# The first chunk's early hidden columns kept in DRAM and multiplied by w_out at the end of layer 1

## The chip, the cores and the metric

The kernel runs on one core of a Trainium2 chip. Its time is the time on the device of one execution, in microseconds (us). A core has five engines that work side by side, each through its own queue in order: TensorE (PE) multiplies matrices, VectorE (DVE) and ScalarE (ACT) work element by element, GpSimd (POOL) does so too, and SyncE (SP) issues the transfers between DRAM and the core's memory (SBUF). PE writes to eight accumulator banks (PSUM). An instruction waits until what it reads is written and what it overwrites is no longer needed; what stands behind it on its queue waits with it.

## The reference

```python
scores = scale * np.matmul(q, k.transpose(0, 1, 3, 2))    # batch 4, heads 8, 576 x 64
Dmat = np.where(rel >= 0, gamma[:, None, None] ** rel[None, :, :], 0.0)
attn = np.matmul(scores * Dmat, v)
x = np.ascontiguousarray(attn.transpose(0, 2, 1, 3)).reshape(B * S, H * D)   # 2304 x 512
g = x @ w_gate                                            # 512 x 1536
x = (g * (1.0 / (1.0 + np.exp(-g))) * (x @ w_val)) @ w_out     # 1536 x 512
h = np.maximum(x @ w_in, 0.0)                             # 512 x 2048
return (h * h) @ w_out2                                   # 2048 x 512
```

A retention without softmax gives 2,304 tokens of 512 channels; two layers follow, a gated one (1,536 hidden columns) and one with a squared ReLU (2,048). The weights arrive as 64-bit floats.

## The kernel before

All tokens stand in SBUF as `xy` (128 partitions, 4 blocks of channels, 2,304 tokens). A matrix product in full precision is made of three fast ones: each operand is split into a rounded part and a rest (`split`: ACT casts the first, DVE subtracts for the second), and `three` multiplies high by high, high by low and low by high.

**Weights.** A 64-bit weight tile of 128 x 512 is a *unit*. `conversion` turns the 68 units into 32 bits, in the order of the list `order`: a load (`raw`), two steps on ACT, four or five on DVE, a store to DRAM (`wst`). `pump` advances it step by step; `ensure` runs it until a wanted unit is there. While the attention runs, `UNITS_EARLY` units are done; behind it `PACE` steps go with each product.

**The attention** takes 16 pairs (batch, two heads) one after the other. A pair n has scores, states, and the outputs of pair n - 2, copied to `xy` by ACT out of one bank `o`; its last 64 tokens go through a piece of a bank `s`. The flag `chain` fixes the order of each engine's instructions there to that of the program, for what is written inside. From pair 6 on each pair also takes one projection (`hidden0`) of the *first chunk*, the first 448 tokens: 12 matmuls for gate or value of one of the first six of twelve column blocks f. The split hidden tiles stay in SBUF (`hs`).

**Layer 1** behind it. `out0` multiplies the six stored hidden tiles by w_out: 72 matmuls into four banks, saved to DRAM as `part`. The other work is done in *passes*. A pass (1, 0), (1, 1), (2, 0), ... takes two blocks of tokens (464 each in layer 1, 384 in layer 2) and multiplies 2 x 2 blocks of weights by 2 x 2 blocks of tokens with seven products in place of eight (`slot` i = 1 to 7, six matmuls each). One such product over two column blocks is a *system* n. The token operands `xo_h`, `xo_l` of product i come from `renew` (sums of blocks of `xy` on DVE, then a split), the weight operands `wi` from `build`: GpSimd makes the sums (`stationary`: s1 and three in place), ACT and DVE split them, and the first pass of a layer stores them as `win` for the later ones. The pass (1, "rest") takes the first chunk with the other six column blocks, by plain products (`plain_slot`, 24 matmuls of 448 columns a system). `out1` and `out2` multiply hidden tiles `ho_hi`, `ho_lo` by w_out tiles `wo` (a pool of four, two to a pair of column blocks; `load_out` loads one and splits it) and add into `xy`.

Outside `chain` a scheduler sets the order on each engine, by its own estimate of times; each engine then runs that order. Before, the passes of layer 1 run (1, 0), "rest", (1, 1); `part` is loaded into `xy` in "rest".

Of the kernel before, what the change touches and what calls it, by code (L numbers as in the profile page):

```python
# [61 lines left out]
def retention_moe_kernel(  # L62
# [64 lines left out]
    order = [(1, what, f) for f in range(HALF) for what in "gv"] + [(1, "o", f) for f in range(HALF)]  # L127
# [164 lines left out]
    hs, gates = {}, {}  # L292

    def hidden0(k):
# [13 lines left out]
        hs[f] = (hi, lo)  # L308

    acc = []  # L310
    part = part_p.tile([P, CC, M0], F32, tag="part", name="part")

    def out0(f):

        if f == 0:
            acc.extend(ps_a.tile([P, 512], F32, tag=f"a{i}", name=f"a{i}")[:, :M0] for i in range(CC))
        ensure((1, "o", f), units)
        w, h = units.pop((1, "o", f)), hs.pop(f)
        for cc in range(CC):
            three(acc[cc], cut(w, cc * P, P), h, f == 0, f == HALF - 1)  # L320
        if f < HALF - 1:
            return
        for cc, a in enumerate(acc):
# [4 lines left out]
            sp.dma_start(out=part[:, cc, :], in_=dst)

    with ExitStack() as st:  # L330
# [11 lines left out]
        pairs = [(b, hp) for b in range(B) for hp in range(NP)]  # L342
# [181 lines left out]
    tt = dve.tensor_tensor  # L524


    passes = list(TOKENS)
    systems = [
        (ph, p, k, what)
        for ph, p in passes  # L530
        for k in range(HALF // 2 if p == "rest" else 0, (F1, F2)[ph - 1] // 2)
        for what in ("gv", "i")[ph - 1]
    ]
    win = {
        (ph, k, what, x): part_p.tile([P, 2, 256 * len(r)], F32, tag=f"win{ph}{what}{k}{x}", name="win")
        for ph, p, k, what in systems if p == 0 for x, r in enumerate(ROWS)
    }
    xo = {}

    def renew(at, i):  # L540


        m = M[at[0]]
        if at[1] == "rest":
            m, src = M0, xy[:, 2 * i - 2:2 * i, :M0]
        else:
            b11, b12, b21, b22 = (xy[:, c:c + 2, t:t + m] for c in (0, 2) for t in TOKENS[at])
            b31, b41 = b11, b21
            if at == (1, 1) and i in (7, 4):
                b31 = b41 = temp("bv", 2)  # L550
            if i == 5:
                tt(out=b12, in0=b12, in1=b11, op=ALU.subtract)
            elif i == 6:
                tt(out=b12, in0=b22, in1=b12, op=ALU.subtract)
            elif i == 7:
                tt(out=b31, in0=b12, in1=b11, op=ALU.subtract)
            elif i == 4:
                tt(out=b41, in0=b21, in1=b12, op=ALU.subtract)
            src = {1: b11, 2: b21, 3: b22, 4: b41, 5: b12, 6: b12, 7: b31}[i]
        hi, lo = (xo_p.tile([P, 2, M[1]], F32R, tag=f"x{x}{i}", name=f"xo_{x}") for x in "hl")  # L560
        xo[i] = hi[:, :, :m], lo[:, :, :m]
        split(*xo[i], src)

    def temp(tag, rows):
        return c4_p.tile([P, rows, M[1]], F32, tag=tag, name=f"c{tag}")

    sys_, built = {}, {}

    inputs = {}

    def load_in(n):
        ph, p, k, what = systems[n]
        inputs[n] = [in_p.tile([P, 512], F32, tag=f"in{x}", name="w_in") for x in range(2)]
        for x, w in enumerate(inputs[n]):
            ensure((ph, what, 2 * k + x), stored)
            sp.dma_start(out=w, in_=wst[ph, what, 2 * k + x])

    def operand_tile(n, x):
        w = wi_p.tile([P, 2, 256 * len(ROWS[x])], F32R, tag=f"wi{x}", name="wi")
        for at, i in enumerate(ROWS[x]):  # L580
            built[n, i] = w[:, :, 256 * at:256 * at + 256]
        return w

    def build(n):

        ph, p, k, what = systems[n]
        if p not in (0, "rest"):
            for x in (0, 3, 2, 1):
                w = operand_tile(n, x)
                sp.dma_start(out=w.bitcast(F32), in_=win[ph, k, what, x])  # L590
                yield
                if x != 2:
                    yield
            return
# [327 lines left out]
```

## Time and profile before

| | us |
|---|---|
| median of 3 runs | 918.2 (915.24 to 922.93) |
| the profiled execution | 920.45 |
| its span, first to last instruction | 918.7 |
| PE busy | 884.8 (96%) |
| DVE busy | 679.3 (74%) |
| ACT busy | 438.6 (48%) |
| POOL busy | 103.3 (11%) |
| transfers, mean rate over the span | 221 GB/s |
| mean granted clock of PE, of 1 | 0.985 |

The busy time of PE is the time in which any matmul was under way. A matmul takes as long again at the lower of PE's two clock levels (1.2 and 2.4 GHz), and counts as busy all the same; the granted clock of a stretch is the mean of the two in parts of the higher. Times below are from the start of the span.

### The profile page before, as it was taken

The page shows a single profiled execution, that of the slowest core. Times are in us where ns is not written, and L with a number is a line of the kernel's source. Part 1 is how long each engine was busy: PE and PEld are TensorE (multiplying, and loading weights), DVE is VectorE, ACT ScalarE, POOL GpSimd, SP SyncE. Part 2 cuts the span into 40 slices and gives each one's busy share as a digit, 9 for nine tenths or more (in the row PEclk, how much of TensorE's full clock was granted, in tenths as well). Part 3 has the DMA queues.
Part 4 walks back from the last instruction along what each step waited for, and adds up shares of the span by engine and source line. Part 5 has one row for each costly group of instructions (what it writes and reads, how often), then busy time and mean ns, then how long its engine had stood idle before and what let it go on. Part 6 is the DMA issues. An engine that isn't in the chain of part 4 may idle for free.

```text
span 918.7 us, 13809 instructions
## 1 busy us (share of the span) xinstructions
PE 884.8 (96%) x5050; PEld 782.0 (85%) x5050; DVE 679.3 (74%) x1098; ACT 438.6 (48%) x781; POOL 103.3 (11%) x119
## 2 busy tenths in 40 slices
PE   7899959899999999899999999999999999999998
PEld 6688848788888899788888999989999999998986
DVE  3777887879989998877877899668754568554553
ACT  3555555675656655455543547534433334243220
POOL 2121160323303000000000223200000000000000
PEclk9999989899999999999999999999999999999999
DMA  8888557998879757889985457534664454554402
GB/s 327 280 277 292 160 196 234 358 318 283 296 258 305 277 190 252 261 302 330 317 289 194 152 200 253 199 140 148 204 197 127 160 171 161 171 184 155 141 3 69
DMA packets 83076, 202.85 MB, mean 221 GB/s; under 512 B 8512, under 2 KB 20288, under 8 KB 83008
## 3 DMA queue, kind: packets, MB, share of 16 engines
q1 hardware_dynamic: 83008, 201.97, 65.3%
q8 instruction: 40, 0.66, 0.3%
q14 instruction: 28, 0.23, 0.1%
HBM read 141.77 MB, written 60.16 MB: 220 GB/s over the span
## 4 chain that ended last, share of the span: by engine, by line
PE 71%; DMA 11%; DVE 10%; issue 3%; ACT 3%; POOL 1%; SPq 1%; ACTq 0%; DVEq 0%; POOLq 0%
PE oacc L116 29%; PE g L116 20%; PE v L116 11%; DMA raw<-in_w 6%; PE z L116 4%; DVE w L116 3%; PE o L116 3%; PE s L116 3%; DVE wi L116 2%; DMA w_in<-wst 1%; DVE xy L116 1%; DMA wst<-w 1%; DMA win<-wi 1%; DVE xo_l L116 1%; DMA kv_sb<-in_kv 1%
## 5 line engine op out<-in xcount | busy, mean ns | idle before, releaser
L116 PE MATMUL g<-xo_h,wi 128*128 128x464 f32 (+2 forms) x816 | 251.1, 359 | 9.4 <-ACT wi L116 3.3
L116 PE MATMUL oacc<-wo,ho_hi 128*128 128x512 f32 x576 | 181.0, 392 | 0.0
L116 PEld LDWEIGHTS g<-xo_h,wi 128*128 128x128 f32 x816 | 153.6, 190 | 23.9 <-ACT cbg L116 4.0
L116 PE MATMUL g<-xo_l,wi 128*128 128x464 f32 (+2 forms) x408 | 146.1, 358 | 0.0
L116 PE MATMUL v<-xo_h,wi 128*128 128x464 f32 (+2 forms) x432 | 136.8, 359 | 7.9 <-ACT wi L116 5.3
L116 PE MATMUL oacc<-ho_hi,wo 128*128 128x464 f32 (+1 forms) x432 | 138.5, 372 | 0.5 <-DVE xy L116 0.5
L116 PEld LDWEIGHTS oacc<-wo,ho_hi 128*128 128x128 f32 x576 | 107.3, 188 | 17.6
L116 DVE TENSOR_TENSOR xy<-oacc,xy 128x464 f32<-128x464 f32 (+2 forms) x146 | 94.3, 650 | 33.8 <-PE oacc L116 33.6
L116 PE MATMUL oacc<-wo,ho_lo 128*128 128x512 f32 x288 | 112.6, 392 | 0.0
L116 PEld LDWEIGHTS v<-xo_h,wi 128*128 128x128 f32 x432 | 80.8, 189 | 15.5 <-ACT wi L116 5.7
L116 PEld LDWEIGHTS oacc<-ho_hi,wo 128*128 128x128 f32 x432 | 81.0, 188 | 10.1 <-DVE xy L116 0.9
L116 DVE TENSOR_SCALAR w<-w 128x512 f32<-128x512 f32 (+1 forms) x136 | 58.6, 431 | 37.2 <-ACT w L116 36.4
L116 PEld LDWEIGHTS g<-xo_l,wi 128*128 128x128 f32 x408 | 77.7, 191 | 6.4
L116 PE MATMUL oacc<-ho_lo,wo 128*128 128x464 f32 (+1 forms) x216 | 80.1, 371 | 0.0
L116 ACT ACTIVATE raw<-raw 128x512 uint32<-128x512 uint16 x68 | 45.9, 675 | 68.6 <-DMA raw<-in_w 62.8
L116 PE MATMUL v<-xo_l,wi 128*128 128x464 f32 (+2 forms) x216 | 77.2, 357 | 0.0
L116 DVE TENSOR_TENSOR wo<-wo 128x512 fp32r<-128x512 f32 x78 | 54.2, 708 | 16.5 <-ACT wo L116 16.3
L116 DVE TENSOR_TENSOR cbg<-v,cbg 128x384 f32<-128x384 f32 (+1 forms) x72 | 41.7, 579 | 30.1 <-ACT cbg L116 19.4
L116 PEld LDWEIGHTS oacc<-wo,ho_lo 128*128 128x128 f32 x288 | 54.1, 188 | 11.5
L116 ACT CAST wo<-wo 128x512 fp32r<-128x512 f32 x78 | 47.4, 622 | 32.5 <-DMA wo<-wst 31.7
L116 ACT CAST wi<-w_in 128x512 fp32r<-128x512 f32 x72 | 44.1, 618 | 38.2 <-POOL w_in L116 9.2
L116 PE MATMUL z<-xo_h,wi 128*128 128x464 f32 (+1 forms) x192 | 61.8, 360 | 0.2 <-DVE cag L116 0.2
(100 smaller groups left out, 1366.6 us busy)
## 6 DMA issues: line engine op xcount, KB each, us to landing
wi<-win SPq DMA_DIRECT2D x84, 512.0 KB, 4.2
raw<-in_w SPq DMA_DIRECT2D x68, 512.0 KB, 5.0
win<-wi SPq DMA_DIRECT2D x60, 512.0 KB, 4.3
wo<-wst SPq DMA_DIRECT2D x78, 256.0 KB, 4.2
wst<-w SPq DMA_DIRECT2D x68, 256.0 KB, 5.2
w_in<-wst SPq DMA_DIRECT2D x52, 256.0 KB, 4.1
qk_sb<-in_qk SPq DMA_DIRECT2D x15, 576.0 KB, 5.8
kv_sb<-in_kv SPq DMA_DIRECT2D x15, 576.0 KB, 4.4
```

The lines of the kernel that those rows point to most:

```text
L116: i = op(*args, **kw)
```

## The change

- `out0`, its banks and `part` go. `hidden0` stores its split tiles to DRAM (`h_st`, two stores of 224 KB for each of the six). In the "rest" pass `early_hidden` loads them back, and `out1` multiplies them there, with 12 more additions or copies into `xy`; their w_out units become ordinary `wo` tiles.
- The passes of layer 1 run (1, 0), (1, 1), "rest". The token blocks change: (1, 0) takes the tokens from 448 and 1,840, (1, 1) those from 912 and 1,376, (2, 0) those from 768 and 1,920, which the "rest" pass does not write.
- The attention takes the batches in the order 0, 3, 1, 2, so that the tokens of (1, 0) are there by pair 13. In pairs 14 and 15 the operands 1 and 5 of the first system are made, in pairs 14 to 17 its weight operands, inside `chain`.
- `WA` 14 to 8, `UNITS_EARLY` 14 to 13, and the 24 steps of conversion between the `out0` go.

```diff
-    (1, 0): (M0 + M[1], M0 + 2 * M[1]),
+    (1, 0): (M0, M0 + 3 * M[1]),
+    (1, 1): (M0 + M[1], M0 + 2 * M[1]),
     (1, "rest"): (0,),
-    (1, 1): (M0, M0 + 3 * M[1]),
-    **{(2, p): (M[2] * p, NT // 2 + M[2] * p) for p in range(NT // (2 * M[2]))},
+    (2, 0): (2 * M[2], 5 * M[2]),
...
+SOON = (1, 5)
+BATCHES = (0, 3, 1, 2)
...
-WA = 14
+WA = 8
...
-UNITS_EARLY = 14
-
-PUMPS = {0: 1, "out": 4}
+UNITS_EARLY = 13
+
+PUMPS = {0: 1}
...
         split(hi, lo, t)
-        hs[f] = (hi, lo)
+        for x, part in enumerate((hi, lo)):
+            sp.dma_start(out=h_st[f // 2, x][:, f % 2], in_=f32(part))
...
-        pairs = [(b, hp) for b in range(B) for hp in range(NP)]
+        pairs = [(b, hp) for b in BATCHES for hp in range(NP)]
...
             if nxt:
                 prep_state(n + 1)
+            if n == 13:
+                load_in(0)
+            if n == 14:
+                make = build(0)
+                renew((1, 0), 1)
+            if n == 15:
+                renew((1, 0), 5)
+            if n >= 14:
+                next(make, None)
+                next(make, None)
+        for _ in make:
+            pass
...
+    def early_hidden(k):
+        parts = [ho_p.tile([P, 2, M0], F32R, tag=f"{x}b", name="ho_e") for x in "hl"]
+        for x, t in enumerate(parts):
+            sp.dma_start(out=t.bitcast(F32), in_=h_st[k, x])
+        hid[rest + 2 * k, "b"] = parts
...
+    for k in range(HALF // 2):
+        plan(rest + 1 + k, rest + 2 * k, "b", k)
+        fetch.setdefault(rest + k, []).append((1, range(2 * k, 2 * k + 2)))
+    for x, (at, n) in enumerate(((4, 1), (5, 3), (6, 5))):
+        plan(rest + at, rest + n, "a")
+        fetch.setdefault(rest + at - 1, []).append((1, range(HALF + 2 * x, HALF + 2 * x + 2)))
...
         if n == 0:
-            load_in(0)
             load_in(1)
-            for _ in build(0):
-                pass
-            seq = [("out", 0), ("out", 1), (1, n), ("out", 2), (5, n), ("out", 3), (6, n), ("out", 4), ("out", 5), (2, n)]
-            for i in (1, 5, 6, 2):
+            for i in (6, 2, 7, 4, 3):
                 renew(passes[0], i)
+            seq = [(1, n), (5, n), (2, n), (6, n)]
...
-        if (n, p) == (systems.index((1, "rest", HALF // 2, "g")) + 1, "rest"):
-            sp.dma_start(out=xy[:, :, :M0], in_=part)
+        if rest <= n < rest + HALF // 2:
+            early_hidden(n - rest)
+        for j in {rest + 3: (5, 6, 3), rest + 4: (7,), rest + 5: (4,)}.get(n, ()):
+            renew((2, 0), j)
```

**The order, first excerpt: ACT ahead of the attention's last banks.** Numbers tell buffers apart; `xy<-o` is the copy of the bank `o`, `raw` and `w<-raw` are the first steps of a unit's conversion, `w_hi` the high part of a weight or hidden tile. Before, from the copy of pair 13's bank to that of pair 14's:

```order
L116 COPY xy_78<-o_1385 128x512
L116 CAST w_hi_1406<-w_1298 128x512
L116 COPY sb_1421<-kvs_1412 128x64
L116 CAST w_hi_1441<-t_1356 128x448
L116 COPY xy_78<-s_1402 128x64
L116 ACTIVATE raw_1296<-raw_1296 128x512
L116 ACTIVATE w_1452<-raw_1296 128x512
L116 COPY xy_78<-o_1455 128x512
```

In the changed kernel, up to the copy of pair 14's bank (`o_1583`):

```order
L120 CAST wi_1749<-w_in_1706 128x512
L120 COPY xy_78<-o_1499 128x512
L120 CAST w_hi_1520<-w_1404 128x512
L120 COPY sb_1535<-kvs_1526 128x64
L120 ACTIVATE raw_1752<-raw_1752 128x512
L120 CAST w_hi_1555<-t_1462 128x448
L120 COPY xy_78<-s_1516 128x64
L120 CAST xo_h_1567<-xy_78 128x928
L120 CAST wi_1573<-s1_1478 128x256
L120 ACTIVATE raw_1402<-raw_1402 128x512
L120 ACTIVATE w_1580<-raw_1402 128x512
L120 COPY xy_78<-o_1583 128x512
```

Between the two copies there now stand, besides what was there, a cast of system 1's weights before them, the first step of the next unit (`raw_1752`), and the casts of operand 5 (`xo_h_1567`) and of a weight sum (`wi_1573`).

**Second excerpt: PE behind the last projection** (`v<-xh, w_hi`; `a0` to `a3` are the banks of `out0`; `g`, `v` and `z` those of the products). Before:

```order
L116 MATMUL v_1532<-xl_601,w_hi_1472 128x448
L116 MATMUL v_1532<-xh_600,w_lo_1473 128x448
L116 MATMUL a0_1710<-w_hi_731,w_hi_1520 128x448
L116 MATMUL a0_1710<-w_lo_732,w_hi_1520 128x448
L116 MATMUL a1_1711<-w_hi_731,w_hi_1520 128x448
L116 MATMUL a1_1711<-w_lo_732,w_hi_1520 128x448
L116 MATMUL a2_1712<-w_hi_731,w_hi_1520 128x448
L116 MATMUL a2_1712<-w_lo_732,w_hi_1520 128x448
L116 MATMUL a3_1713<-w_hi_731,w_hi_1520 128x448
L116 MATMUL a3_1713<-w_lo_732,w_hi_1520 128x448
L116 MATMUL g_1766<-xo_h_1688,wi_1669 128x464
L116 MATMUL g_1766<-xo_l_1689,wi_1669 128x464
```

In the changed kernel, where six matmuls of system 1 (`g_1806` with `wi_1749`) also stand ahead of the attention's last `s` bank, and five of `g_1737` ahead of these rows:

```order
L120 MATMUL g_1737<-xo_h_1474,wi_1480 128x464
L120 MATMUL v_1759<-xo_h_1567,wi_1573 128x464
L120 MATMUL v_1759<-xo_l_1568,wi_1573 128x464
L120 MATMUL v_1759<-xo_h_1567,wi_1573 128x464 x2
L120 MATMUL v_1759<-xo_l_1568,wi_1573 128x464
L120 MATMUL v_1759<-xo_h_1567,wi_1573 128x464
L120 MATMUL z_1768<-xo_h_1715,wi_1480 128x464
L120 MATMUL g_1806<-xo_h_1711,wi_1798 128x464
L120 MATMUL g_1737<-xo_h_1711,wi_1631 128x464
L120 MATMUL g_1737<-xo_l_1712,wi_1631 128x464
L120 MATMUL g_1737<-xo_h_1711,wi_1631 128x464 x2
L120 MATMUL g_1737<-xo_l_1712,wi_1631 128x464
```

The matmuls of `out0` are gone; products 1 and 5 of system 0 follow the projection, and then products 2 and 6 begin, whose operands are `xo_h_1715` and `xo_h_1711`, `xo_l_1712`.

**Third excerpt: PE in the "rest" pass,** `oacc` being the banks of `out1`. Before, from the last matmul of `wo_3418`, whose place `wo_3794` takes; that one is first used 47 rows later:

```order
L116 MATMUL oacc_3703<-ho_hi_3522,wo_3418 128x464
L116 MATMUL oacc_3703<-ho_hi_3522,wo_3422 128x464
L116 MATMUL oacc_3703<-ho_lo_3523,wo_3422 128x464
L116 MATMUL oacc_3703<-ho_hi_3522,wo_3422 128x464
L116 MATMUL oacc_3736<-ho_hi_3595,wo_3635 128x448
L116 MATMUL oacc_3736<-ho_lo_3596,wo_3635 128x448
L116 MATMUL oacc_3736<-ho_hi_3595,wo_3635 128x448
L116 MATMUL oacc_3736<-ho_hi_3595,wo_3639 128x448
L116 MATMUL oacc_3736<-ho_lo_3596,wo_3639 128x448
L116 MATMUL oacc_3736<-ho_hi_3595,wo_3639 128x448
L116 MATMUL g_3848<-xo_h_3334,wi_3817 128x448 x2
L116 MATMUL g_3848<-xo_l_3335,wi_3817 128x448
```

In the changed kernel, right behind the last matmul of `wo_4784`, whose place `wo_4917` takes:

```order
L120 MATMUL oacc_5112<-ho_hi_4884,wo_4788 128x464
L120 MATMUL oacc_5112<-ho_lo_4885,wo_4788 128x464
L120 MATMUL oacc_5112<-ho_hi_4884,wo_4788 128x464
L120 MATMUL g_5272<-xo_l_4676,wi_5195 128x448
L120 MATMUL g_5272<-xo_h_4675,wi_5195 128x448 x2
L120 MATMUL g_5272<-xo_l_4676,wi_5195 128x448
L120 MATMUL g_5272<-xo_h_4675,wi_5195 128x448
L120 MATMUL g_5272<-xo_h_4711,wi_5195 128x448
L120 MATMUL g_5272<-xo_l_4712,wi_5195 128x448
L120 MATMUL g_5272<-xo_h_4711,wi_5195 128x448 x2
L120 MATMUL g_5272<-xo_l_4712,wi_5195 128x448
L120 MATMUL oacc_5120<-ho_e_4925,wo_4917 128x448
```

The tile that takes a freed place is now wanted 12 rows later.

## Rows read from the trace of the kernel before

**Rows 1.** Stretches behind the attention: PE, PEld, DVE, ACT, POOL busy (count), PEclk, DMA, GB/s.

```profile
118.55:164.46 45.91, 34.93 (x151) 28.82 (x151) 37.24 (x56) 24.27 (x45) 15.54 (x10) 0.89 0.69 227
164.46:189.56 25.10, 21.77 (x92) 18.97 (x92) 22.84 (x34) 16.99 (x33) 10.18 (x11) 0.86 1.01 351
189.56:288.55 98.99, 98.48 (x470) 87.62 (x468) 88.98 (x148) 59.94 (x106) 25.70 (x27) 1.00 0.84 288
288.55:364.90 76.35, 74.40 (x358) 66.72 (x357) 72.93 (x117) 43.43 (x69) 2.62 (x3) 1.00 0.77 255
364.90:402.39 37.49, 34.88 (x160) 31.01 (x159) 29.95 (x52) 19.29 (x33) 0.00 (x0) 0.95 0.83 285
402.39:523.79 121.40, 120.76 (x578) 107.92 (x576) 95.20 (x161) 63.45 (x109) 5.89 (x7) 1.00 0.76 261
523.79:918.70 394.91, 390.29 (x1945) 351.69 (x1943) 250.82 (x366) 149.06 (x255) 21.38 (x24) 1.00 0.47 157
```

**Rows 2.** Chain that ended last: start, duration, what, matmuls.

```profile
338.92 2.44 PE v L116 x12
...
486.00 2.51 PE g L116 x12
```

**Rows 3.** PE in order of time: start, duration, instruction, idle before and its releaser.

```profile
113.50 0.87 PE L116 MATMUL o<-qs,sb 64*64 64x128 f32 x12
...
118.19 0.36 PE L116 MATMUL v<-xh,w_lo 128*128 128x448 f32 x1
...
134.25 0.76 PE L116 MATMUL v<-xo_h,wi 128*128 128x464 f32 x1 [5.27 <-ACT wi L116]
...
169.31 0.75 PE L116 MATMUL g<-xo_h,wi 128*128 128x464 f32 x1 [3.33 <-ACT wi L116]
...
383.21 0.76 PE L116 MATMUL g<-xo_h,wi 128*128 128x464 f32 x1 [2.61 <-ACT cbg L116]
```

**Rows 4.** ACT in order of time, at the end of the attention.

```profile
101.76 0.91 ACT L116 ACTIVATE kv_sb<-kv_sb,ks_sb 128x256 f32<-128x256 f32 x2
...
109.24 0.56 ACT L116 CAST w_hi<-t 128x448 fp32r<-128x448 f32 x1 [3.45 <-DVE t L116]
...
110.97 0.57 ACT L116 COPY xy<-o 128x512 f32<-128x512 f32 x1
...
115.92 3.57 ACT L116 CAST xo_h<-xy 128x928 fp32r<-128x928 f32 x4
```

**Rows 5.** DVE in order of time, same stretch.

```profile
102.74 1.22 DVE L116 TENSOR_TENSOR p_sb<-s,mask_sb 128x1024 f32<-128x1024 f32 x1 [1.57 <-PE s L116]
...
108.59 0.61 DVE L116 TENSOR_TENSOR t<-v,t 128x448 f32<-128x448 f32 x1
...
111.05 1.12 DVE L116 TENSOR_TENSOR xy<-xy 128x928 f32<-128x928 f32 x1
...
116.93 3.73 DVE L116 TENSOR_TENSOR xo_l<-xy,xo_h 128x928 fp32r<-128x928 f32 x3 [1.49 <-ACT xo_h L116]
```

**Rows 6.** Groups by shape: count, busy us, mean ns, idle before.

```profile
L116 DVE TENSOR_TENSOR wi<-w_in,wi 128x512 fp32r<-128x512 f32 x72 | 52.8, 738 | 3.1 <-ACT wi L116 2.8
...
L116 ACT ACTIVATE raw<-raw 128x512 uint32<-128x512 uint16 x68 | 45.9, 675 | 68.6 <-DMA raw<-in_w 62.8 <-DVE cag L116 2.2 <-DVE xy L116 1.6
...
L116 POOL TENSOR_TENSOR w_in<-w_in 128x256 f32<-128x256 f32 x40 | 38.9, 973 | 11.7 <-DMA w_in<-wst 9.1
```

**Rows 7.** SP issuing transfers, in order of time.

```profile
94.65 0.33 SPq L116 DMA_DIRECT2D kv_sb<-in_kv  x1
...
104.63 0.33 SPq L116 DMA_DIRECT2D raw<-in_w  x1
```

**Rows 8.** Transfers on the page: count, size, median us from issue to landing.

```profile
raw<-in_w SPq DMA_DIRECT2D x68, 512.0 KB, 5.0
...
wo<-wst SPq DMA_DIRECT2D x78, 256.0 KB, 4.2
```

**Rows 9.** POOL in order of time, behind the attention.

```profile
125.29 5.36 POOL L116 TENSOR_TENSOR w_in<-s,w_in 128x256 f32<-128x256 f32 x1 [4.03 <-DVE wi L116]
```

More of the change, by code (lines that the diff above doesn't have):

```diff
@@ L126, in retention_moe_kernel @@
     units = {}
[L127 removed]
+    order = [(1, what, f) for f in range(HALF) for what in "gv"]
     plain = len(order)
+    order += [(1, "o", f) for f in range(HALF)]
     for k in range(HALF // 2, F1 // 2):
@@ L290, in project @@
         return ps
-    hs, gates = {}, {}
+    gates = {}
+    h_st = {
+        (k, x): part_p.tile([P, 2, M0], F32, tag=f"h{k}{x}", name="h_st")
+        for k in range(HALF // 2) for x in range(2)
+    }
     def hidden0(k):
@@ new lines, in temp, with load_in, operand_tile @@
+    def temp(tag, rows):
+        return c4_p.tile([P, rows, M[1]], F32, tag=tag, name=f"c{tag}")
+    built = {}
+    inputs = {}
+    def load_in(n):
+        ph, p, k, what = systems[n]
+        inputs[n] = [in_p.tile([P, 512], F32, tag=f"in{x}", name="w_in") for x in range(2)]
+        for x, w in enumerate(inputs[n]):
+            ensure((ph, what, 2 * k + x), stored)
+            sp.dma_start(out=w, in_=wst[ph, what, 2 * k + x])
+    def operand_tile(n, x):
+        w = wi_p.tile([P, 2, 256 * len(ROWS[x])], F32R, tag=f"wi{x}", name="wi")
+        for at, i in enumerate(ROWS[x]):
+            built[n, i] = w[:, :, 256 * at:256 * at + 256]
+        return w
@@ new lines, in build, with to @@
+    def build(n):
+        ph, p, k, what = systems[n]
+        if p not in (0, "rest"):
+            for x in (0, 3, 2, 1):
+                w = operand_tile(n, x)
+                sp.dma_start(out=w.bitcast(F32), in_=win[ph, k, what, x])
+                yield
+                if x != 2:
+                    yield
+            return
+        w0, w1_ = inputs.pop(n)
+        later = []
+        def to(x, src):
+            w = operand_tile(n, x)
+            split(w[:, 0], w[:, 1], src)
+            if p == 0:
+                later.append((win[ph, k, what, x], w.bitcast(F32)))
+        if p == "rest":
+            to(0, w0)
+            for _ in range(5):
+                yield
+            to(2, w1_)
+            return
+        s1 = in_p.tile([P, 256], F32, tag="s1", name="s1", bufs=1)
+        for _ in stationary(w0, w1_, s1, to):
+            yield
+            for dst, w in later:
+                sp.dma_start(out=dst, in_=w)
+            later.clear()
@@ L523, in retention_moe_kernel @@
     late = True
[L524 to L594, printed above, removed]
-        w0, w1_ = inputs.pop(n)
-        later = []
-        def to(x, src):
-            w = operand_tile(n, x)
-            split(w[:, 0], w[:, 1], src)
-            if p == 0:
-                later.append((win[ph, k, what, x], w.bitcast(F32)))
-        if p == "rest":
-            to(0, w0)
-            for _ in range(5):
-                yield
-            to(2, w1_)
-            return
-        s1 = in_p.tile([P, 256], F32, tag="s1", name="s1", bufs=1)
-        for _ in stationary(w0, w1_, s1, to):
-            yield
-            for dst, w in later:
-                sp.dma_start(out=dst, in_=w)
-            later.clear()
+    sys_ = {}
@@ L726, in out_bank, with out1 @@
         return ps_a.tile([P, 512], F32, tag=f"a{1 + turn['o'] % 3}", name="oacc")
-    def out1(n, which, cc):
-        ph, p, k, what = systems[n]
+    def out1(n, which, cc, k=None):
+        ph, p, k0, what = systems[n]
+        k = k0 if k is None else k
         m = M0 if p == "rest" else M[ph]
```

102 lines of the change are left out of this document (55 added, 47 removed).

## Prediction

> **What bounds the kernel now.** The page's busy shares say little here, since TensorE (PE) also counts as busy at half clock. So I cut the span into stretches and set PE's time in each against its work [rows 1]. Full pace is 2.51 us for 12 matmuls of 464 columns, 0.2092 us each, and 2.44 us for 12 of 448, 0.2033 us each [rows 2]. The attention's last projection starts its last matmul at 118.19 and ends near 118.55 [rows 3]. From there to 523.79, where layer 2 begins on PE, the instruction order holds 1,506 matmuls of 464 columns, 288 of 448 and 6 of 384 (1.0 us): 315.1 + 58.5 + 1.0 = 374.6 us of work in 405.2 us. So 30.6 us are lost in layer 1. By stretch: to 189.56 it is 168 and 72 matmuls, 49.8 us of 71.0, **21.2 lost**; to 288.55 another 1.1; to 523.79 another **8.4**. Layer 2 loses 4.6 us (394.91 less 390.29 busy) and is not touched. Elsewhere PE is at its pace; 30.6 us is all that another order can win there.
>
> The 21.2 are idle time (11.0 and 3.3) and half clock behind it (granted 0.89 and 0.86, against 1.00 in the next stretch) [rows 1]. The PE rows name the waits: 5.27 us for ACT's `wi` at 134.25 and 3.33 us at 169.31, both for operands of the first systems [rows 3]. VectorE (DVE) is busy 37.2 of 45.9 and 22.8 of 25.1 us there, and 89.0 of 99.0 us in the stretch behind: the second limit, right under PE.
>
> **The change: matmuls.** The order counts the same matmuls in both kernels, form by form. The 72 of `out0` leave the start of layer 1 and return as `out1` in the "rest" pass: 72 × 0.2033 = 14.6 us of filler go from the place where operands are late to one where PE has work. Cost on PE: nothing; what counts is which waits remain.
>
> **The attention until pair 13.** The twelve stores `h_st` go through SP's queue; in every second pair the second one waits for DVE's `w_lo` and stands ahead of the next `kv_sb` load. The last such load was issued at 94.65 [rows 7] and its data were used at 101.76 [rows 4]. It now stands behind two stores and two `w_in` loads, some 2.5 us later. With seven microseconds between issue and use I take 0.5, and up to 5 us if each of these pairs waits one.
>
> **The end of the attention (first order excerpt).** Now `renew` of operands 1 and 5 and the first builds stand between the last pairs. I follow the queues with the rows' durations. ACT scales `kv_sb` from 101.76 for 0.91, then makes `xo_h` (3.57/4 = 0.89) to about 103.6. DVE, which began `p_sb` at 102.74 [rows 5], has `xo_l` (3.73/3 = 1.24) and a `wi` (0.74, [rows 6]) ahead of it, so `p_sb` starts at 105.6, 2.8 late; with one more `wi` the product `t` is 3.5 late, done at 112.7 instead of 109.2. ACT now has the conversion of `raw_1752` ahead of `w_hi`; SP issues that load behind DVE's late step, near 108 instead of 104.63 [rows 7], and with 5.0 us to landing [rows 8] it is there at 113. Then in line: the conversion's first step 0.7 [rows 6], `w_hi` 0.56, `w_lo` 0.6, the subtraction for operand 5 (1.12), `xo_h` 0.89, `wi` 0.4, two steps of the next conversion 1.3, and only then the copy of the attention's bank `o`: done near 119, where it was 110.97 + 0.57 = 111.5 [rows 4]. There is one such bank. PE started its next use at 113.50 [rows 3] and must now wait until 119: **5.4 us** lost. Bounds: 0, if the additions fit into ACT's idle 3.45 us at 109.24 and DVE's small gaps; 9, if the load lands late as well.
>
> **After the attention (second excerpt).** The last projection ends at 118.55 + 5.4 + 6 matmuls of system 1 (1.25) = 125.2. PE then has 15 matmuls whose operands exist (3.1 us, to 128.3). The next one needs `xo_l_1712`, 18 DVE instructions behind the one that ended near 117.7. The mean DVE instruction from 118.55 to 288.55 takes 149.1 us / 238 = 0.626 us [rows 1], so 11.3 us, with the longer ones here 130: a wait of 1.7. The next 39 matmuls (8.2 us) meet `xo_l_1726`, 12 long DVE instructions (10.2 us) later: a wait of 2. For half clock I add 2.5: the stretch of the 3.33 us wait has 90 matmuls in the order (18.8 us) and took 25.1, so 3.0 went besides the idle time. Sum 5.4 + 3.7 + 2.5 = **11.6 us where 21.2 were lost**. Bounds 4 to 18.
>
> **Pass (1,0) behind that.** It loses its filler, but keeps its vector work: 23 weight units (22 before) must be converted ahead of its last systems, and the next pass's operands come right behind. From the fifth system to the second of the next pass the order has 582 matmuls of 464 columns (121.8 us) and 199 DVE instructions (× 0.626 = 124.6 us). So DVE is as long as PE, where it had a tenth to spare. PE loses 2.8 if DVE never idles and 17 if it idles as it did from 189.56 to 288.55 (10.1%: 124.6/0.899 = 138.6). I take **4**, near the lower end, since DVE idles mostly when PE is what it waits for.
>
> **The "rest" pass at the change of layer (third excerpt).** `wo` has four tiles. `wo_4917` takes the place of `wo_4784`, whose last matmul now stands 13 matmuls (2.6 us) ahead of the first one that needs the new tile. Issue 0.4, landing 4.2 [rows 8] and ACT's cast 0.6 make 5.2: a wait of 2.6 us, and up to 1.8 for half clock, as behind the 2.61 us wait at 383.21 [rows 3] (below). I take **4**, bounds 0 to 8. The other pairs have 40 to 80 rows between. Eight more additions on DVE (0.61 each, as `t` in [rows 5]) and four fewer ACT copies lie beside the pass's matmuls, which have grown by 14.6 us.
>
> **The other 9.5 us of before.** From 288.55 to 364.90 the order has 171 and 186 matmuls, 73.6 of 76.35 us: 2.8 lost at the change from (1,0) to "rest", now counted under (1,0). From there to 402.39 it has 129 and 30, 33.1 of 37.5 us: 4.4 lost, nearly all in one place, where ACT copies a PSUM bank late (2.61 idle at 383.21, 1.8 of half clock behind it) [rows 3]. Conversions go on as before, but at other places; I keep half, 2.2, and the remaining 2.3 as they are: **4.5**.
>
> **Sum.** 0.5 + 11.6 + 4 + 4 + 4.5 = 24.6 lost, against 30.6: a gain of 6. The profiled execution took 920.45 us (span 918.7), 0.2% over the median of 918.2. Off the median: **912 us**.
>
> **Rivals.** (a) *The additions fit.* ACT's 3.45 us of idle time take its share, `raw` lands early, DVE never stops: losses 3.7 + 2.8 + 3 = 9.5, a gain of 21, 897 us; with half of its advantage over the forecast 905. For it: ACT is busy only 24.3 of 45.9 us after the attention. Against: queues run in order, and one bank holds PE.
>
> (b) *VectorE becomes the bound* in pass (1,0), from its third pair of systems to its end. At the idle share of 118.55 to 288.55 (20.9 of 170.0 us, 12.3%) the stretch takes 142.1 and loses 20.3 instead of 4: total 40.9, 10 us slower, 928 us. It breaks even at an idle share of 5.5% (131.8 us, 10 lost) and is 1% slower from 11.6%. For it: 10.1 and 12.3% are what the trace has. Against: PE was full for most of that, so part of the idle time was DVE waiting for PE.
>
> (c) *The gap only moves*: 7 us at the bank `o`, 3.7 behind it, 2.5 of half clock, 6 in the pass, 7 in "rest" and 4.4 make 30.6: no change, 918 us.
>
> (d) *GpSimd's part is blocked.* One of its subtractions took 5.36 us at 125.29 [rows 9], while DVE ran without a gap, against a mean of 0.97 [rows 6]. Eight such now stand beside the last pairs, and ACT's `wi_1779` waits for the fifth, ahead of the last bank copies. One block on that path costs 4.4 us: 916 us. The Trainium skill (SBUF — State Buffer, Who interferes with whom) has a rule for this: a vector instruction with two SBUF inputs and a GpSimd instruction that reads SBUF use the same ports, and whichever is first holds them for its whole length. By that rule all eight could be hit, since DVE is dense there, and the row of 5.36 us agrees.
>
> **Chances.** Forecast (907 to 916) 0.38; (a) 0.27; (b) 0.15; (c) 0.12; (d) 0.08. The range leaves out the far third of (a) and the far half of (b), together less than two in ten: 899 to 926. About 1% (9 us) is what a measurement of this kernel can tell from no change. Faster by over 1%: (a) and a third of the forecast, 0.40; slower by over 1%: most of (b), 0.13; within: 0.47.
>
> **What would show it.** Right: PE idle for 4 to 6 us ahead of the attention's last `o`, released by ACT's `xy`; two waits of 1 to 2 us behind the last projection; a wait for `wo` in "rest"; DVE busy above 93% in pass (1,0). Wrong: PE without a gap where the attention ends (then (a)); PE waiting again and again for DVE or ACT, with a granted clock under 1.00, through pass (1,0) (then (b)); or pairs slower than 7 us each before 100 because `kv_sb` is late.

## The result and the profile after

The changed kernel takes **924.8 us** (median of ten runs, 922.45 to 925.88), the kernel before, run beside it, 917.5: a ratio of 1.0071 (95% interval 1.0053 to 1.0090). It is 0.7% slower, where 912 was forecast. The spans of the two profiled executions are 922.9 and 918.7, 4.2 us apart; the rest of the 7.3 us between the medians comes from the profile of before, which lay 2.9 us over its median.

First the stretches of the changed kernel, as in [rows 1] (busy time and instructions of PE, PEld, DVE, ACT, POOL; granted clock, DMA share, GB/s):

```profile
100.00:128.54 28.54, 20.44 (x191) 16.73 (x191) 20.71 (x32) 16.77 (x34) 8.09 (x10) 0.88 0.46 158
128.54:200.00 71.46, 69.53 (x328) 60.98 (x327) 67.03 (x104) 47.19 (x85) 17.47 (x16) 1.00 0.90 310
200.00:309.00 109.00, 97.37 (x432) 79.84 (x430) 95.62 (x154) 57.06 (x96) 22.01 (x24) 0.98 0.81 267
309.00:400.00 91.00, 90.78 (x431) 80.65 (x432) 76.20 (x129) 50.28 (x86) 0.00 (x0) 1.00 0.89 302
400.00:411.00 11.00, 9.15 (x43) 7.52 (x42) 7.64 (x16) 4.79 (x9) 0.00 (x0) 1.00 0.76 270
411.00:552.10 141.10, 141.09 (x689) 128.19 (x688) 120.51 (x199) 69.57 (x117) 11.63 (x14) 1.00 0.69 230
552.10:922.90 370.80, 366.17 (x1824) 329.57 (x1823) 227.16 (x333) 140.34 (x241) 17.87 (x18) 1.00 0.48 158
```

At full pace 432 matmuls of 464 columns are 90.4 us: from 200 to 309, in pass (1, 0), PE loses **18.6 us**. Before, the same pass from 190 to 303 held 527 matmuls in 113 us and lost 2.8 (the row below). VectorE is busy 95.6 of 109, so it idles 12.3%. The stretch ahead of 200 loses 2.8 (328 matmuls), the two from 309 to 411 lose 0.8 and 2.0 (431 and 43), and the change of layer behind them under 1. (A matmul that a boundary cuts is counted on both sides, so these come out a little low.) By the counts of the order, from 128.54 to the last matmul of layer 1 at 552.1 the work is 397.2 us of 423.6: 26.4 lost, and the attention ends 8.9 us later. That is 35.3 against 30.6 before; layer 2 is as it was. The stretch of the kernel before:

```profile
190.00:303.00 113.00, 111.16 (x527) 98.10 (x525) 103.27 (x170) 71.06 (x123) 26.07 (x27) 1.00 0.86 295
```

The end of the attention, PE in order of time:

```profile
108.56 0.33 PE L120 MATMUL s<-qs,sb 64*64 64x64 f32 x4 [1.85 <-DVE pl L120]
...
109.09 0.87 PE L120 MATMUL o<-qs,sb 64*64 64x128 f32 x12
...
109.89 1.09 PE L120 MATMUL o<-p_sb,kv_sb 128*64 128x128 f32 x16
...
115.97 0.33 PE L120 MATMUL s<-qs,sb 64*64 64x64 f32 x4 [2.36 <-ACT xy L120]
...
120.46 1.55 PE L120 MATMUL o<-qs,sb 64*64 64x128 f32 x12 [3.89 <-ACT xy L120]
...
121.94 1.98 PE L120 MATMUL o<-p_sb,kv_sb 128*64 128x128 f32 x16
...
128.33 0.37 PE L120 MATMUL v<-xh,w_lo 128*128 128x448 f32 x1
```

Three waits, 8.1 us, and behind the third the lower clock (1.55 and 1.98 where the same groups took 0.87 and 1.09). The last projection's last matmul starts at 128.33; without the six matmuls of system 1 that now stand ahead of it (1.25) it is 8.9 later than at 118.19 [rows 3]. What ACT, which copies `o` and `s` to `xy`, did meanwhile, and the load that it waited for:

```profile
105.96 0.58 ACT L120 COPY xy<-o 128x512 f32<-128x512 f32 x1
...
114.60 0.67 ACT L120 ACTIVATE raw<-raw 128x512 uint32<-128x512 uint16 x1 [5.95 <-DMA raw<-in_w]
...
119.75 0.57 ACT L120 COPY xy<-o 128x512 f32<-128x512 f32 x1
```

```profile
108.28 0.43 SPq L120 DMA_DIRECT2D raw<-in_w  x1
```

ACT stood 5.95 us at the first step of a unit whose load was issued at 108.28. Behind it stood the casts and the copy at 119.75, for which PE waited until 120.46.

In pass (1, 0) PE waits many times for a little; two of them, and then VectorE's main wait in that stretch (us in total, times, longest):

```profile
213.16 0.47 PE L120 MATMUL oacc<-ho_hi,wo 128*128 128x464 f32 x1 [1.82 <-ACT ho_hi L120]
...
269.65 0.48 PE L120 MATMUL g<-xo_h,wi 128*128 128x464 f32 x1 [2.48 <-ACT cbv L120]
```

```profile
DVE w L120 <- ACT w L120: 9.4, 8, 2.4
```

`w` is what ACT makes of a unit that has just landed. One turn of a unit through one of the two `raw` buffers reads so: VectorE's last step frees the buffer, SP issues the next load at once, ACT waits for it, VectorE for ACT:

```profile
232.17 0.68 DVE L120 CUSTOM_DVE_ANT_0 w<-raw,w 128x1024 uint16<-128x1024 uint16 x1
...
232.88 0.33 SPq L120 DMA_DIRECT2D raw<-in_w  x1
...
238.64 0.67 ACT L120 ACTIVATE raw<-raw 128x512 uint32<-128x512 uint16 x1 [3.67 <-DMA raw<-in_w]
...
239.89 0.43 DVE L120 TENSOR_SCALAR w<-w 128x512 f32<-128x512 f32 x1 [2.43 <-ACT w L120]
```

Twenty such loads on, from the 16th to the 36th, the last one that the pass needs:

```profile
134.52 0.40 SPq L120 DMA_DIRECT2D raw<-in_w  x1
...
282.85 0.33 SPq L120 DMA_DIRECT2D raw<-in_w  x1
```

148.3 us for twenty: 7.4 us a unit, so each of the two buffers is held 14.8 us at a time, of which the load shown is some 5.7. In the kernel before, also with two buffers:

```profile
140.07 0.33 SPq L116 DMA_DIRECT2D raw<-in_w  x1
...
276.37 0.33 SPq L116 DMA_DIRECT2D raw<-in_w  x1
```

That is 6.8 us a unit, so the conversion was hardly faster there, and the 36th load went out only 6.5 us earlier. What differs is that PE spent 14.6 us on `out0` and lost 21.2 us before it came to the systems that need these units; now it comes to them sooner (328 matmuls of 464 columns from 128.54 to 200, against 168 up to 189.56 before).

At the change of layer the expected wait isn't there. The last matmuls of a first early pair of columns, the loads of the next pair's `wo`, VectorE's split of the second of them, and their first use on PE:

```profile
499.49 2.61 PE L120 MATMUL oacc<-ho_e,wo 128*128 128x448 f32 x12
...
501.98 1.20 SPq L120 DMA_DIRECT2D wo<-wst  x1
...
503.74 0.38 SPq L120 DMA_DIRECT2D wo<-wst  x1
...
508.78 0.69 DVE L120 TENSOR_TENSOR wo<-wo 128x512 fp32r<-128x512 f32 x1 [0.89 <-ACT wo L120]
...
511.62 2.60 PE L120 MATMUL oacc<-ho_e,wo 128*128 128x448 f32 x12
```

The two tiles take the places that these matmuls leave, not those of `wo_4784` and its neighbour; they are loaded and split by 509.47, two microseconds ahead of their use at 511.62.

### The profile page after: what moved, and what is told of

Its sections match the earlier page's. It is cut to its first block, busy times and chain, and to the rows that moved or that the text cites. A ratio compares the mean times of both kernels' runs of the same rounds, so it can differ in the third digit from the quotient of the medians.

```text
span 922.9 us, 13859 instructions
## 1 busy us (share of the span) xinstructions
PE 886.7 (96%) x5050; PEld 778.7 (84%) x5050; DVE 682.7 (74%) x1106; ACT 436.6 (47%) x781; POOL 97.5 (11%) x119
## 4 chain that ended last, share of the span: by engine, by line
PE 73%; DMA 11%; DVE 10%; ACT 3%; issue 2%; SPq 1%; POOL 0%; ACTq 0%; DVEq 0%; POOLq 0%
PE oacc L120 32%; PE g L120 20%; PE v L120 11%; DMA raw<-in_w 6%; PE z L120 4%; DVE w L120 4%; PE o L120 2%; PE s L120 2%; DVE xy L120 2%; DMA wst<-w 2%; DMA w_in<-wst 2%; DMA wo<-wst 1%; DVE wi L120 1%; DMA kv_sb<-in_kv 1%; ACT raw L120 1%
## 5 line engine op out<-in xcount | busy, mean ns | idle before, releaser
L120 PE MATMUL g<-xo_l,wi 128*128 128x384 f32 (+2 forms) x408 | 145.2, 356 | 1.1 <-DVE xo_l L120 1.1
L120 DVE TENSOR_TENSOR xy<-oacc,xy 128x464 f32<-128x464 f32 (+2 forms) x154 | 99.5, 649 | 38.9 <-PE oacc L120 38.7
L120 DVE TENSOR_TENSOR wo<-wo 128x512 fp32r<-128x512 f32 x84 | 56.9, 689 | 19.7 <-ACT wo L120 19.6
L120 ACT CAST wo<-wo 128x512 fp32r<-128x512 f32 x84 | 51.2, 622 | 40.8 <-DMA wo<-wst 40.6
L120 DVE TENSOR_TENSOR cbg<-v,cbg 128x384 f32<-128x384 f32 (+1 forms) x72 | 41.8, 580 | 30.8 <-ACT cbg L120 20.9
L120 POOL TENSOR_TENSOR s<-w_in 128x256 f32<-128x256 f32 x20 | 19.9, 995 | 354.7 <-DMA w_in<-wst 331.4
```

Source lines behind the costliest of these rows:

```text
L120: i = op(*args, **kw)
```

## The experiments

The kernel before was run with each set, and its median went from 916.2 to 919.6; so ratios to it are compared, and a difference between two kernels is that of their ratios times 917.5. With the 95% intervals of both ratios such a difference is known to some 3 or 4 us. "Loss" is PE's from 200 to 309 us: 109 less 0.2092 for each matmul in the row. The changed kernel: ratio 1.0071, loss 18.6.

**Three raw buffers** (`a_raw3`).

```diff
-    raw_p = pool(mid, "raw_p", 2)
+    raw_p = pool(mid, "raw_p", 3)
...
-            if loads["pool"] < 2:
+            if loads["pool"] < 3:
```

> The changed kernel with three raw buffers in place of two. Theory 1 (the conversion of weights paces pass (1,0): each of two buffers is held some 14 us, from the issue of its load to the last VectorE step, so a unit takes 7.2 us where PE would need one in about 5.7): PE's loss between 200 and 309 us falls from 19.0 to under 9, the loads 15 to 36 take under 135 us in place of 150, and the time falls to 910 to 916. Theory 2 (VectorE's own work is the bound of the pass): VectorE has nothing less to do, the loss stays within 3 us of 19.0 and the time at 922 to 926. Theory 3 (the wait is for PSUM banks and copies, not for weights): no change either.

Measured 910.4 us, ratio 0.9925 (0.9897 to 0.9953): 13.4 us less than the changed kernel, and faster than before. The stretch, and the loads 16 and 36:

```profile
200.00:309.00 109.00, 103.60 (x478) 89.85 (x477) 104.32 (x168) 62.72 (x105) 18.80 (x21) 0.98 0.90 308
```

```profile
134.18 1.41 SPq L120 DMA_DIRECT2D raw<-in_w  x1
...
256.97 0.33 SPq L120 DMA_DIRECT2D raw<-in_w  x1
```

Loss 9.0 (at the edge of what theory 1 gave), 6.1 us a unit, VectorE 96% busy. Theory 1 holds in its size; what it left out is that VectorE is then nearly full. The second and third theories, by which a third buffer does nothing, fall as sole causes.

**The matmuls of out0 cut short in the kernel before** (`b_no_out0`).

```diff
-        for cc in range(CC):
-            three(acc[cc], cut(w, cc * P, P), h, f == 0, f == HALF - 1)
+        if f == 0:
+            for cc in range(CC):
+                three(acc[cc], cut(w, cc * P, P), h, True, True)
```

> The kernel before with the matmuls of out0 left out but for the first hidden tile's 12 (so that the first chunk's output lacks five of its six early tiles); conversions and everything else stay. 60 matmuls, 12.2 us of PE's work, are gone. If they were cover for a pass that the conversion of weights paces (theory 1), less than 6 us of it comes back: 912 to 917. If the work was a cost like any other there, 904 to 907.

920.6 us, ratio 1.0035 (1.0017 to 1.0053): slower, with 12 us less work, which neither expectation has. PE's row says why:

```profile
164.95 0.76 PE L116 MATMUL z<-xo_h,wi 128*128 128x464 f32 x1 [13.51 <-ACT part_sb L116]
```

The copies of `out0`'s banks go through a `raw` buffer, and `z` uses one of these banks. With the matmuls done early PE stood at that copy (I take it that the copy waited for a buffer, behind conversions). This run tells nothing of the cover; the next one leaves the copies out as well:

**out0 gone altogether** (`b_out0_gone`).

```diff
...
-        for cc in range(CC):
-            three(acc[cc], cut(w, cc * P, P), h, f == 0, f == HALF - 1)
-        if f < HALF - 1:
-            return
-        for cc, a in enumerate(acc):
...
-            sp.dma_start(out=part[:, cc, :], in_=dst)
...
-            sp.dma_start(out=xy[:, :, :M0], in_=part)
```

> The kernel before without out0: its 72 matmuls, its eight copies and stores and the load of part are gone (the first chunk's output lacks those columns); the conversions between them stay. Theory 1 (the matmuls were cover there, since conversion and VectorE set the pace of pass (1,0)): at most 5 of the 14.6 us come back, 912 to 918. If they cost their full time there: 902 to 904.

908.7 us, ratio 0.9920 (0.9890 to 0.9951): 7.3 of the 14.6 us come back, between the two expectations. The other half is waited away later, as in this stretch (114 matmuls, 23.8 us, in 30):

```profile
230.00:260.00 30.00, 26.83 (x114) 21.91 (x114) 27.67 (x46) 15.17 (x27) 8.10 (x8) 0.94 0.75 247
```

**The early products left out of the changed kernel's rest pass** (`a_no_early`).

```diff
-        plan(rest + 1 + k, rest + 2 * k, "b", k)
```

> The changed kernel without the products of the early hidden tiles in the rest pass (72 matmuls of 448 columns, 12 additions or copies into xy; the first chunk's output lacks those columns). If PE is the bound of the rest pass, all 14.6 us come back: 909 to 911. If VectorE or the weights bound it, under 8: 917 to 921.

907.5 us, ratio 0.9906 (0.9876 to 0.9936): 15.1 us less than the changed kernel. In their new place the 72 matmuls cost all of their time, as far as the two intervals tell. In this trace the attention also ends earlier, with the projection's last matmul at 123.51 where it was 128.33, so that a part of the 15.1 may come from there.

**UNITS_EARLY 14 in the changed kernel** (`a_units14`).

```diff
-UNITS_EARLY = 13
+UNITS_EARLY = 14
```

> The changed kernel with UNITS_EARLY 14, as before: the load of the 14th unit and ACT's first step on it stand in the fixed order of the last pairs, not ahead of the copies of the attention's last banks. If this step of ACT, which waits for a load that lands at 114.5, holds the copies and so the bank o (my prediction's step), the 6.2 us that PE waits for ACT's xy at 115.97 and 120.46 fall to under 3, and the time to 918 to 922. If the operands made beside the pairs hold them (casts of operand 5 and of a weight sum), the waits stay over 5 and the time is 923 to 926.

920.3 us, ratio 1.0031 (1.0008 to 1.0054): 3.7 us less. ACT doesn't wait for a load ahead of the copies any more, and of the 6.2 us that PE waited for `xy` one wait of 3.07 is left, just over the 3 expected:

```profile
116.94 1.54 PE L120 MATMUL o<-qs,sb 64*64 64x128 f32 x12 [3.07 <-ACT xy L120]
```

So the scheduler's early placing of one step of ACT was about half of what PE waited for `xy`. I take the casts made beside the pairs for the other half; no run separates them. The 3.7 us are a sum of more than that. The projection's last matmul starts at 124.59 where it was 128.33, the loss from 200 to 309 is 13.4 where it was 18.6 (457 matmuls), and from 411 to 480 PE does 311 matmuls where it did 330, some 4 us less work. The 36th load goes out at 270.92, 6.6 us a unit behind the 16th at 138.42: with two buffers too, a turn is not one fixed time.

**The first operands written behind the attention** (`a_ops_behind`).

```diff
-            if n == 13:
-                load_in(0)
-            if n == 14:
-                make = build(0)
-                renew((1, 0), 1)
-            if n == 15:
-                renew((1, 0), 5)
...
-            for i in (6, 2, 7, 4, 3):
+            load_in(0)
+            for _ in build(0):
+                pass
+            for i in (1, 5, 6, 2, 7, 4, 3):
```

> The changed kernel with the first system's operands and weight operands written behind the attention instead of inside the pairs 13 to 17, as they were before the change; the scheduler may place them. If making them beside the pairs pays, PE's idle time moves behind the attention and the time is 926 to 935. If it costs as much as it brings (8.7 us at the attention's end against some 10 behind it), the time is 922 to 927. If the pass is paced by the conversion of weights (theory 1), an early start of PE is waited away anyway: within 3 us of 924.8.

931.5 us, ratio 1.0151 (1.0118 to 1.0184). But it isn't the undoing that it was meant to be: freed of the fixed order, the scheduler placed operands among earlier pairs, where ACT's casts of 0.96 us stand now and VectorE's subtractions behind them, and PE waits there:

```profile
92.32 0.96 ACT L120 CAST xo_h<-xy 128x928 fp32r<-128x928 f32 x1
...
99.73 0.56 ACT L120 CAST w_hi<-t 128x448 fp32r<-128x448 f32 x1 [5.41 <-DVE t L120]
...
100.46 0.48 PE L120 MATMUL s<-qk_sb 64*64 64x64 f32 x4 [4.17 <-ACT xy L120]
```

**The same in fixed order, with UNITS_EARLY 14** (`a_ops_last`): `build(0)` and `renew` of 1 and 5 behind the last pair, inside `chain`. Their lines inside the pairs go as above, but `load_in(0)` stays at pair 13.

```diff
...
         pump(PUMPS[0])
+        for _ in build(0):
+            pass
+        renew((1, 0), 1)
+        renew((1, 0), 5)
```

> The changed kernel with UNITS_EARLY 14 and the first system's operands (products 1 and 5, all weight operands) written behind the last pair, still in fixed order: a clean undoing of making them beside the last pairs, against 920.3 with them there. If that placing gains what it was worked out to gain, PE stands idle 8 to 12 us more behind the attention and 3 to 5 less at its end: 925 to 930. If pass (1,0) is paced by VectorE and the raw buffers, a later start of PE is made up in the pass: 918 to 923.

927.5 us, ratio 1.0106 (1.0072 to 1.0140), 6.9 us more than with the operands beside the pairs (`a_units14`). From 128 to 200 only 273 matmuls were done, where `a_units14` did 325, at a granted clock of 0.89:

```profile
128.00:200.00 72.00, 64.66 (x273) 55.86 (x274) 63.81 (x97) 46.47 (x82) 23.97 (x21) 0.89 0.85 309
```

From 200 to 309 it then did 480, a loss of 8.6 where `a_units14` lost 13.4: a part of the late start is made up in the pass. Making the operands beside the pairs gains, as the change meant it to, even though it costs at the attention's end.

**More work for VectorE** (`a_dve_extra`).

```diff
             act.copy(a[:, 0], x)
+            if (ph, p) == (1, 0) and n > 1:
+                for _ in range(2):
+                    tt(out=extra, in0=a[:, 0], in1=a[:, 0], op=ALU.mult)
...
             act.copy(b[:, 0], x)
+            if (ph, p) == (1, 0) and n > 1:
+                tt(out=extra, in0=b[:, 0], in1=b[:, 0], op=ALU.mult)
```

> The changed kernel with 30 more multiplications on VectorE in pass (1,0), of 128 x 464 into a tile of their own, three in each system from the third on: 30 x 0.55 = 16.5 us of VectorE. Theory 2 (VectorE's work is the bound of the pass): the time grows by 12 to 17, to 937 to 942. Theory 1 (VectorE idles 12% there because it waits for loads into two raw buffers): a part falls into its idle time, growth 2 to 9, 927 to 934.

936.9 us, ratio 1.0242 (1.0201 to 1.0283): 15.7 us more, about as much as the added work of 16.5, and the growth that theory 2 gave.

```profile
200.00:309.00 109.00, 91.17 (x374) 74.91 (x373) 95.95 (x159) 51.16 (x88) 21.08 (x24) 0.91 0.75 246
```

Loss 30.8. Theory 1 as I had put it is wrong here: none of the added work fell into VectorE's idle time. VectorE is busy 88%, as without the additions. Over some 760 matmuls behind the projection it is idle 18.3 us here (125.73 to 319.14) and 17.8 in the changed kernel (128.68 to 308.56). Its idle time is no room: its steps are themselves a part of each buffer's turn, and what stands ahead of them in the queue lengthens the turn. The loads 16 and 36 went out at 131.77 and 290.27, 7.9 us a unit where it was 7.4. So neither theory holds alone: VectorE's steps and the two buffers make one loop, and work added to it or a buffer added to it both move the time.

**Both gains together** (`a_raw3_u14`): three buffers from the start and UNITS_EARLY 14.

> The changed kernel with both single edits that gained: three raw buffers and UNITS_EARLY 14. If the two losses are separate places (the conversion in pass (1,0), 14 us, and ACT's early step at the attention's end, 4.5 us), the gains add: 904 to 908. If the later start was merely waited away in the pass anyway, 909 to 912.

909.8 us, ratio 0.9924 (0.9897 to 0.9951), no gain over three buffers alone.

```profile
200.00:309.00 109.00, 104.64 (x489) 90.81 (x488) 106.11 (x172) 66.62 (x113) 19.22 (x21) 1.00 0.90 311
```

Loss 6.7. With a third buffer free, the scheduler again put ACT's step on the next unit ahead of the last copies, and ACT stood there for 6.15 us until 113.42. So it doesn't test whether the gains add.

**The third buffer only behind the attention** (`r_gate`): UNITS_EARLY 14, and a buffer from the memory that the attention leaves.

```diff
-UNITS_EARLY = 13
+UNITS_EARLY = 14
...
-            if loads["pool"] < 2:
...
+            if loads["pool"] < 2 or third and not third[0]:
...
     early.close()
     parts.close()
+    third.extend((0, pool(mid, "raw4_p", 1)))
```

> UNITS_EARLY 14, and the third raw buffer taken only behind the attention, from memory that the attention held: no load can be issued early into it, so that ACT's step on the 15th unit no longer stands ahead of the attention's last copies, where it waited until 113.42 with three buffers open from the start. If the start of PE still counts, the attention's end gives back 4 us: 904 to 907. If VectorE, busy 97% from 128 to 309 us with three buffers, sets the end of pass (1,0) in any case, only what VectorE itself waited (4 us at 114.57) can come back: 907 to 911.

**906.1 us**, ratio 0.9889 (0.9865 to 0.9913), the fastest of the kernels that do all of the work: 1.1% under before, 1.8% under the changed kernel. Against `a_units14`, from which it differs only in that buffer, it is 13.0 us faster: so the gain of a third buffer in the pass needs no earlier loads during the attention. Of PE's waits for `xy` in the attention one of 1.53 us is left:

```profile
116.17 0.87 PE L120 MATMUL o<-qs,sb 64*64 64x128 f32 x12 [1.53 <-ACT xy L120]
```

```profile
200.00:309.00 109.00, 105.06 (x487) 91.63 (x486) 105.01 (x171) 63.97 (x107) 19.30 (x19) 0.98 0.88 307
```

The loss in the pass is as with three buffers from the start, 7.1 where it was 9.0 (`a_raw3`) and 6.7 (`a_raw3_u14`), and the projection's last matmul starts at 122.40 where it started at 128.33 in the changed kernel. So the start of PE seems to count still. The time is only some 3 us under those two, at the edge of the intervals.

**Fewer steps for VectorE** (`r_less_dve`).

```diff
-        ts(out=wf, in0=wf, scalar1=TINY, scalar2=HUGE, op0=ALU.max, op1=ALU.min)
+        if whole:
+            ts(out=wf, in0=wf, scalar1=TINY, scalar2=HUGE, op0=ALU.max, op1=ALU.min)
...
-        ts(out=w, in0=w, scalar1=3, ...
+        if whole:
+            ts(out=w, in0=w, scalar1=3, ...
```

> The kernel with three raw buffers and UNITS_EARLY 14, with two of VectorE's four steps on a unit left out from the 15th unit on (the bounds on the exponent and the shift with its mask, so that these weights are wrong): 0.83 us a unit, 18 us of VectorE's work between 128 and 309 us. If VectorE's work is the next bound right behind the raw buffers, PE's 12.2 us of loss there fall to under 5 and the time to 898 to 903. If not, 906 to 911.

903.5 us, ratio 0.9856 (0.9824 to 0.9889), against 0.9924 with all steps (`a_raw3_u14`): 6.2 us less.

```profile
200.00:309.00 109.00, 108.59 (x516) 96.49 (x515) 101.38 (x154) 69.39 (x117) 18.27 (x20) 1.00 0.93 333
```

Loss 1.1. The time missed its bound by half a microsecond; the loss in this stretch is gone. Behind the third buffer VectorE's work is the next limit, and in this stretch no further one shows. The two steps are also a part of each buffer's turn (5.4 us a unit here, 6.3 in `a_raw3_u14`), so this run alone doesn't part the two; that VectorE was busy 97% with three buffers speaks for its work.

**One of VectorE's steps on GpSimd** (`r_pool_step`), for the units 15 to 36 of `r_gate`.

```diff
-        ts(out=wf, in0=wf, scalar1=TINY, scalar2=HUGE, op0=ALU.max, op1=ALU.min)
+        (ts if early else pool_e.tensor_scalar)(out=wf, in0=wf, scalar1=TINY, ...
```

> The best kernel so far (906.1: the third raw buffer behind the attention, UNITS_EARLY 14), with one of VectorE's four steps on a unit, the bounds on the exponent, made by GpSimd for the units 15 to 36, those of pass (1,0): VectorE has 22 x 0.46 = 10 us less to do where it is 97% busy, and GpSimd, busy 19 of 109 us there, 22 steps more. If VectorE's work paces the pass and the two engines do not hinder each other, PE's loss from 200 to 309 falls from 7.4 to under 4 and the time to 901 to 904. If they do (GpSimd's subtractions took up to 5.36 us beside a dense VectorE), or a step on GpSimd is so slow that it holds the raw buffers again, 906 to 915.

915.2 us, ratio 0.9960 (0.9937 to 0.9983), 6.5 us slower than `r_gate`. The groups from 128 to 309 us of GpSimd's step and of VectorE's next one, and VectorE's own form of the step in `r_gate` (count, busy us, mean ns, idle before):

```profile
L120 POOL TENSOR_SCALAR w<-w 128x512 f32<-128x512 f32 x22 | 48.8, 2220 | 45.8 <-ACT w L120 42.5 <-DVE xy L120 3.3
...
L120 DVE TENSOR_SCALAR w<-w 128x512 uint32<-128x512 uint32 x28 | 14.0, 504 | 5.7 <-POOL w L120 5.7
```

```profile
L120 DVE TENSOR_SCALAR w<-w 128x512 f32<-128x512 f32 x27 | 12.5, 461 | 1.0 <-ACT w L120 1.0
```

A step that took VectorE 0.46 us takes GpSimd 2.22, and the buffer is held meanwhile. VectorE lost 5.7 us waiting for it.

## Why the prediction was wrong, point by point

- **The matmuls: "Cost on PE: nothing; what counts is which waits remain."** The frame was right: the loss moved from 30.6 to 35.3, and the spans differ by 4.2. But the filler was half free where it stood (7.3 of 14.6 came back without it) and cost about all of its time where it went (15.1): the move by itself is worth some 7.8 us against the change, worked out from two runs that leave work out and known to some 4 us. Without these matmuls in either place the two kernels differ by 1.3 us (0.9920 and 0.9906), which is no difference by the intervals.
- **The attention until pair 13, 0.5.** PE shows no wait for `kv_sb`. The late load is there all the same: ACT waited 1.61 us for the last one, ahead of the copy at 105.96.

```profile
102.12 0.91 ACT L120 ACTIVATE kv_sb<-kv_sb,ks_sb 128x256 f32<-128x256 f32 x2 [1.61 <-DMA kv_sb<-in_kv]
```

- **The end of the attention and behind it, 11.6.** Right in size (11.7) and nearly in place: the projection ends 8.9 us later, with 8.1 us of waits and 1.6 of half clock in it, and 2.8 are lost from 128.54 to 200. The sum is partly luck, since the parts were off: I had put 5.4 at the bank `o`, and it is three waits of 8.1, while the waits behind the projection were 0.5 to 0.7 us each, not 2. The working's cause, ACT's step on a load that lands "at 113" (114.6), is about half of it by `a_units14`. The copy that I had done "near 119" started at 119.75.
- **Pass (1, 0): "I take 4, near the lower end, since DVE idles mostly when PE is what it waits for."** This is the step that failed: 18.6. The bound above it, 17 at an idle share of 10.1%, and rival (b)'s 20.3 at 12.3% were the better numbers, and VectorE idled 12.3%. It waited for ACT's `w`, 9.4 of its 13.4 us, which waited for loads. So the reason I gave fails: of VectorE's idle time 0.8 us was waiting for PE. I had counted the units to convert and priced them in VectorE's time only; the turn of two buffers, 14.8 us each, was in no term, and a third buffer took 13.4 us off the time. Rival (b) came near in time (928) and half in mechanism: VectorE's work does set the pace (`a_dve_extra`), but what kept it idle were mostly loads into two buffers, and it was nearly full, at 96%, only when a third had come.
- **The "rest" pass, 4.** Nothing. The premise that `wo_4917` takes the place of `wo_4784` was mine, counted four tiles back, and it was wrong; the loads went out at 501.98 and 503.74, when the two tiles ahead of it were done. Two microseconds were to spare.
- **The other 9.5, of which 4.5 kept.** Some 5, as taken.
- **Rival (d).** GpSimd's eight instructions beside the last pairs took 0.72 to 1.50 us; none was blocked for long. **Rivals (a)** and **(c)** had the additions fit, or the gap move; PE did wait at the attention's end, and the loss that decided lies a hundred microseconds later.

What the change was to bring, it brought: at the attention's end and from there to 200 PE loses 11.7 us (8.9 and 2.8), where 21.2 were lost, and `a_ops_last` puts 6.9 us on the operands made beside the pairs. It was given back in pass (1, 0), where the loop of loads, conversion and free buffer sets the pace and the filler had hidden a part of it. With a third buffer in the right place the changed kernel is 1.1% faster than before. A third buffer in the kernel before was not run. Beside the stored hidden tiles there is no room for it, but behind the last `out0` (its last matmul starts at 163.57) their memory comes free, and a third buffer would fit. So it stays open how much of these 1.1% is the change and how much the buffer alone.

## What to carry to other kernels

Before filler (work that PE does while operands are late) is taken out of a stretch, look for the slower thing that it hid: here the issue times of one kind of load, twenty of them, gave 7.4 us a unit and two buffers held 14.8 us each, and the kernel before, at 6.8, was hardly faster. Idle time of an engine that works in order is not room for more: find what ends it, since added work there lengthened the loop by about its full length. Where a scheduler may move instructions into a queue, one step that waits for a late load holds all behind it; a buffer whose memory only comes free at the right time keeps such a load back.

## What the runs showed of the hardware that I had not expected

VectorE's subtraction `wi<-w_in,wi`, 128 x 512, takes 0.69 us alone and 1.22 beside GpSimd, while its addition out of an accumulator bank, `xy<-oacc,xy`, takes 0.63 beside GpSimd too. In the changed kernel (VectorE's rows, then those of GpSimd at the same times):

```profile
229.86 0.69 DVE L120 TENSOR_TENSOR wi<-w_in,wi 128x512 fp32r<-128x512 f32 x1 [0.68 <-ACT wi L120]
...
244.87 0.63 DVE L120 TENSOR_TENSOR xy<-oacc,xy 128x464 f32<-128x464 f32 x1
...
251.07 1.22 DVE L120 TENSOR_TENSOR wi<-w_in,wi 128x512 fp32r<-128x512 f32 x1
...
244.04 1.50 POOL L120 TENSOR_TENSOR w_in<-w_in 128x256 f32<-128x256 f32 x1
...
250.94 0.80 POOL L120 TENSOR_TENSOR w_in<-s,w_in 128x256 f32<-128x256 f32 x1
...
251.82 1.07 POOL L120 TENSOR_TENSOR w_in<-w_in 128x256 f32<-128x256 f32 x1
```

The Trainium skill (SBUF — State Buffer, Who interferes with whom) has it so: a vector instruction with at most one SBUF input, outside VectorE's 2-port modes, isn't hindered by GpSimd, and one with two is by a GpSimd instruction that reads SBUF. These rows agree. And one elementwise step with two constants, 128 x 512, took GpSimd 2.22 us on the mean (`r_pool_step`) against VectorE's 0.46 (`r_gate`), nearly five times as long.
